# Attention with pooled queries: another spread of the value products over the steps, and two turning steps moved

## The chip, the core and the metric

The kernel runs on one core of a Trainium2 chip. The metric is the device time of one execution in microseconds (us), as the median of several runs. TensorE (PE) multiplies matrices into PSUM, VectorE (DVE), ScalarE (ACT) and GpSimd (POOL) work element by element, and SyncE (SP) issues the DMAs. Each engine takes its own instructions in the order of the program and waits on semaphores for what it needs from the others.

## The reference

Attention is followed by a dense layer and a layer of eight experts; the change touches the attention alone.

```
q_pool = q.reshape(B, H, S // 2, 2, D).mean(axis=3)       # B 2, H 8, S 1152, D 64
scores = (1 / sqrt(D)) * q_pool @ k.T                     # 576 x 1152 for each head
attn   = softmax(scores)                                  # row maximum taken off, divided by row sums
x      = (attn @ v), heads side by side                   # 1152 x 512
x      = mish(x @ w_in) @ w_out                           # hidden size 2048
P      = exp(x @ w_gate), then 8 rounds of rows and columns divided by their sums
out    = sum over e of P[:, e] * (relu(x @ w1[e]) @ w2[e])
```

All is float32. The kernel splits operands into a high and a low part and adds two or three products of the parts.

## The kernel before

**Pairs and steps.** The 16 heads are worked in 8 pairs (`p` from 0 to 7). A pair has 2 x 576 = 1152 pooled query rows, that is nine tiles of 128 (`t` from 0 to 8); the middle tile, t = 4, holds rows of both heads. One pass of the loop `for g in range(...)` (L686) is one step, g = 9 p + t; below, "step t" is the step of that number in any pair. A step works on three query tiles at once:

- `scores(g)` (L443): TensorE multiplies the tile's queries with the keys, six matmuls of 384 columns (twelve in step 4) into the one buffer `psS` (three PSUM banks). VectorE then negates, moves the result to a tile `e` and takes the row minimum in the same instruction (L458). So the next step's scores wait until that instruction has ended. `e` has three buffers.
- `exps(g)` (L472) on ScalarE, at the end of the step. One step later `hand_over` (L478) has SP copy `e` to a tile `er` of another format by DMA; the buffer of `e` is free again only when that DMA has landed.
- `transposes(g - 3)` (L535): nine transposes of the tile `er` of three steps before, three to a PSUM buffer `psT` (there are four); ScalarE copies each as the high part `eth` (L538), VectorE writes the low part `etl` (L541).

**Products with the values.** The turned tiles are gathered in four groups of a pair, 256, 320, 320 and 256 queries. A group is full after the transposes of step 4, of step 7, of step 0 of the next pair and of step 2 of the next pair. A full group puts 18 matmuls into the list `av_todo` (L556); `run_av(n)` issues up to n of them. All groups use the one buffer `psA`. With the last of the 18 comes the emptying: a copy on ScalarE (`avt`, L565) and a sum on VectorE (`xs`, L570); until the sum has ended, the next group's first product waits. In pairs 1 to 7 the table `AV` (L612) says how many products a step issues ahead of its transposes and how many behind them (only those that were listed before the step's own transposes); in pair 0 each step issues up to nine, behind the transposes.

**Turning keys and queries.** The table `TURN` (L613) says in which steps TensorE turns keys and queries to the layout that scores need. `trans_k` (L386) turns a third of one head's keys: three transposes to a `psT` buffer, and a copy on ScalarE (L392). Step numbers under `k0` are for the next pair's first head, under `k1` for the pair's own second head, which scores need from step 4 on (in pair 0 `k10` holds instead of `k1`). `trans_q` (L428) turns up to four query tiles: the transposes, a copy on ScalarE (`qT`, L435), and then, listed in `loads` and so issued by SP at the beginning of the next step, the two DMAs of `swap` (L426), which put the halves of the 128 partitions the other way round into a second slot. Under `q` stand the steps of its three parts: the first, of tiles 0 to 3, is done for the next pair, whose step 0 reads it, the other two for the pair's own. Every query tile is used in both slots: the first matmul of a tile's scores reads the first slot, the second one the swapped slot.

**Order within a step** (L692 to L726): listed loads; `scores`; GpSimd's splitting of the next heads (`prep`); the first turning item, if there is one; the first part of the products; the transposes; the hand-over of the step before; the second part of the products; the other turning items; `exps`. ScalarE and VectorE get their copies and sums in the same order.

**Beside it**, DMAs load the next heads' q, k and v (`qraw`, `kraw`, `vraw`) and the weights of the dense layer, whose splitting on VectorE, ScalarE and GpSimd is planned by step number. After 72 steps the dense layer and the experts follow, in which TensorE has work nearly all the time.

Of the kernel before, what the change touches and what calls it, by code (L numbers as in the profile page):

```python
# [23 lines left out]
def pool_attention_mish_sinkhorn_kernel(  # L24
# [22 lines left out]
    NPAIR = B * H // 2  # L47
# [57 lines left out]
    def run(t, eng, most=99):  # L105

        q = queue[eng]
        while q and q[0][0] <= t and most > 0:
            q.pop(0)[1]()
            most -= 1  # L110
# [180 lines left out]
    with ExitStack() as actx:  # L291
        def pool(name, bufs, **kw):
            return actx.enter_context(tc.tile_pool(name=name, bufs=bufs, **kw))
# [27 lines left out]
        for i in range(2):  # L321
            t = z_p.tile([P, 2, 2, P], F32R, name=f"qz{i}")
# [25 lines left out]
        def split_kv(p, j, which, eng, part, more=True):  # L348
            if p == NPAIR:
                return  # L350
            raw = raws[which, p, j]
            pl, dst = (kst_p, kst) if which == "k" else (vst_p, vst)
            if part == 0:
                t = dst[p, j] = pl.tile([P, NK, 2, D], F32R, tag=which + "st", name=f"{which}st{p}_{j}")
                split_hi(eng, t[:, :, 0, :], raw)
            else:
                t = dst[p, j]
                split_lo(eng, t[:, :, 1, :], raw, t[:, :, 0, :])
                p, j = (p, 1) if j == 0 else (p + 1, 0)
                if more and p < NPAIR:  # L360
                    loads.append(lambda: load_kv(p, j, which))
# [24 lines left out]
        def trans_k(p, j, c3):  # L386
            if c3 == 0:
                kT[p, j] = kt_p.tile([P, S], F32R, tag="kT", name=f"kT{p}_{j}")
            ps = ps_t.tile([P, 4, P], F32R, tag="t", name=f"psk{p}_{j}_{c3}")
            for i in range(3):  # L390
                nc.tensor.transpose(ps[:, i, :], kst[p, j][:, 3 * c3 + i].rearrange("p a d -> p (a d)"), identr)  # L391
            nc.scalar.activation(  # L392
                kT[p, j][:, c3 * TH:(c3 + 1) * TH],
                ps[:, 0:3, :].bitcast(F32).rearrange("p a d -> p (a d)"), AF.Copy)
# [15 lines left out]
        def trans_q0(u):  # L410

            n = min(2, QTL - 2 * u)
            ps = ps_t.tile([P, 2, 2, P], F32R, tag="t", name=f"psq0_{u}")
            for i in range(n):
                for s in range(2):
                    nc.tensor.transpose(
                        ps[:, i, s, :], qst[0][:, 2 * u + i, s:s + 2, :].rearrange("p a d -> p (a d)"), identr)
            t, i = q_tile(0, 2 * u)
            nc.scalar.activation(t[:, i:i + n], ps[:, 0:n].bitcast(F32), AF.Copy)
            if 2 * u <= MID < 2 * u + n:  # L420
                middle(0, ps[:, MID - 2 * u], 2)
# [6 lines left out]
        def trans_q(p, u):  # L428
            ps = ps_t.tile([P, 4, P], F32R, tag="t", name=f"psq{p}_{u}")
            t, _ = q_tile(p, 4 * u)  # L430
            n = min(4, QTL - 4 * u)
            for i in range(n):
                nc.tensor.transpose(
                    ps[:, i, :], qst[p][:, 4 * u + i, 0:2, :].rearrange("p a d -> p (a d)"), identr)
            nc.scalar.activation(t[:, :, 0, :], ps[:, 0:n].bitcast(F32), AF.Copy)  # L435
            loads.append(lambda: swap(t))
            if 4 * u == MID:
                middle(p, ps, 1)
                loads.append(lambda: swap(qz[p % 2]))
# [22 lines left out]
        def exps(g):  # L462
            p, t = divmod(g, QTL)
            sc, nm = scS.pop(g)
            sc = sc.rearrange("p a b -> p (a b)")
            if g < 2:
                e = erS[g] = er_p.tile([P, S], F32, tag="er", name=f"er{g}")
            else:
                e = eS[g] = sc
            if t == 0:  # L470
                rsS[p] = tiny.tile([P, QTL], F32, tag="rs", name=f"rs{p}", bufs=2)
            nc.scalar.activation(e, sc, AF.Exp, bias=nm, scale=-1.0, accum_out=rsS[p][:, t:t + 1])  # L472
# [115 lines left out]
        def run_av(n):  # L588
            for _ in range(n):
                if av_todo:  # L590
                    av_todo.pop(0)()

        NQ = NPAIR * QTL
# [15 lines left out]
            "k00": 3, "k01": 4, "k10": 7, "k11": 8,  # L609
        }  # L610
        PREP0 = {"k00": 3, "k01": 3, "q0": 4, "q1": 4, "q2": 5, "q3": 5, "v10": 5, "v11": 7, "k10": 7, "k11": 8}
        AV = [(0, 9), (0, 8), (0, 8), (2, 7), (0, 4), (7, 4), (0, 6), (8, 0), (0, 9)]  # L612
        TURN = {"k0": (5, 6, 7), "k1": (2, 3, 3), "k10": (0, 0, 2), "q0": (2, 2, 3), "q": (6, 1, 2)}  # L613

# [8 lines left out]
        q0, q1, q2 = slice(0, 2), slice(2, 4), slice(4, QTL)  # L625
# [36 lines left out]
        def prep(p, t):  # L662
            for x, at_ in (PREP if p else PREP0).items():
                if at_ == t:
                    if x[0] == "q":
                        split_q(p + 1, nc.gpsimd, int(x[1]))
                    else:
                        split_kv(p + (x[0] == "k"), int(x[1]), x[0], nc.gpsimd, int(x[2]))

        def turn(p, t):  # L670
            fs = []
            for j in range(2):
                pp = p + (j == 0)
                if pp < NPAIR:
                    fs += [
                        lambda pp=pp, j=j, c=c: trans_k(pp, j, c)
                        for c in range(3) if TURN["k10" if p == 0 and j == 1 else f"k{j}"][c] == t]
            for u in range(3):
                pp = p + (u == 0)
                if p == 0 and TURN["q0"][u] == t:  # L680
                    fs.append(lambda u=u: trans_q0(u + 2))
                if 0 < pp < NPAIR and TURN["q"][u] == t:
                    fs.append(lambda pp=pp, u=u: trans_q(pp, u))
            return fs

        for g in range(T0 + EARLY):  # L686
            p, t = divmod(g, QTL)
            if g == 1:
                bctx.close()
                ps_t = pool("ps_t", 4, space=PSUM)  # L690
                ps_a = pool("ps_a", 1, space=PSUM)
            pre = turn(p, t) if g < NQ else []  # L692
            waiting, loads[:] = loads[:], []
            for f in waiting:
                f()
            if g < LAG:
                exps(g)
                for f in pre:
                    f()
                if g + 1 < LAG:  # L700
                    split_kv(0, 0, "v", nc.gpsimd, g)
                    scores(g + 2, ps_s)
            else:
                if LAG < g < NQ:
                    scores(g)
                if p and g < NQ:
                    prep(p, t)
                if g < T0:
                    run(g, "dve")
                if pre:  # L710
                    pre.pop(0)()
                spread = 0 < p < NPAIR
                if spread:
                    run_av(AV[t][0])
                ready = len(av_todo)
                if g < NQ + LAG:
                    transposes(g - LAG)
                if g <= NQ:
                    hand_over(g - 1)
                if not p:  # L720
                    prep(p, t)
                run_av(min(ready, AV[t][1] if spread else 9 if g < NQ else 18))
                for f in pre:
                    f()
                if g < NQ:
                    exps(g)  # L726
            if p and t == 0:
                row_sums(p - 1)
            if p and t == 1:
                turn_sums(p - 1)  # L730
            if late:
                late.pop(0)()
            if g < T0:
                run_all(g)
            if g == QTL:
                load_gate()
            if g == NQ - 1:
                sctx.close()
                ps_o = ctx.enter_context(tc.tile_pool(name="ps_o", bufs=3, space=PSUM, side="right"))
                wpools["d0"] = ctx.enter_context(tc.tile_pool(name="wd0", bufs=1, side="right"))  # L740
                mctx = ExitStack()
                wpools["d1"] = mctx.enter_context(tc.tile_pool(name="wd1", bufs=1, side="right"))
                wpools["t"] = mctx.enter_context(tc.tile_pool(name="wt2", bufs=3, side="right"))
            if g >= T0:
                mish_step(g - T0)
# [50 lines left out]
    for s in range(NS):  # L796
        for th in range(NTH):
            last = max(k for k, b in enumerate(BANKS) if b[:2] == (s, th))
            ready = max(last + 2, NB - 1 if s == NS - 1 else 9 if s == 1 else 0)
# [492 lines left out]
```

## Time and profile before

| | |
|---|---|
| median of 3 runs | 1235.37 us (1233.79 to 1235.45) |
| the profiled execution | 1235.16 us, of which its span 1233.3 us |
| TensorE, busy share of the span | 98% |
| VectorE, ScalarE, GpSimd | 69%, 48%, 51% |
| attention, first to last scores | 6.65 to 263.7 us |
| one pair of heads, steps 0 to 8 (pairs 1 to 6) | 32.1 to 35.0 us |

The span runs from the first to the last instruction; the run's time has 1.9 us more. Over the whole span TensorE is the engine with the least room, but in the attention, the first fifth, three engines are near 85 to 92% busy (TensorE, VectorE, ScalarE), and the DMA engines near 78%. There the chain of waits goes from one engine to another within each step, so the place to look at is the step and not the share.

### The profile page before, as it was taken

The page shows a single profiled execution, that of the slowest core. Times are in us where ns is not written, and L with a number is a line of the kernel's source. Part 1 is how long each engine was busy: PE and PEld are TensorE (multiplying, and loading weights), DVE is VectorE, ACT ScalarE, POOL GpSimd, SP SyncE. Part 2 cuts the span into 40 slices and gives each one's busy share as a digit, 9 for nine tenths or more (in the row PEclk, how much of TensorE's full clock was granted, in tenths as well). Part 3 has the DMA queues.
Part 4 walks back from the last instruction along what each step waited for, and adds up shares of the span by engine and source line. Part 5 has one row for each costly group of instructions (what it writes and reads, how often), then busy time and mean ns, then how long its engine had stood idle before and what let it go on. Part 6 is the DMA issues. An engine that isn't in the chain of part 4 may idle for free.

```text
span 1233.3 us, 19334 instructions
## 1 busy us (share of the span) xinstructions
PE 1209.1 (98%) x6840; PEld 1114.4 (90%) x6840; DVE 854.4 (69%) x1588; ACT 596.9 (48%) x1364; POOL 623.7 (51%) x704
## 2 busy tenths in 40 slices
PE   8999999999999999999999999999999999999998
PEld 8988888989999999898888899998888899998887
DVE  7888889876534433777866767866866767866865
ACT  7888888878454443452322333333322333333331
POOL 5545565415444422374755665555455565555452
PEclk9999999999999999999999999999999999999999
DMA  6877777654222311011111111111111111111112
GB/s 203 278 255 259 254 263 258 221 188 130 86 86 72 97 34 30 1 52 25 39 49 53 46 49 52 52 52 31 37 45 52 51 45 52 53 52 34 39 39 77
DMA packets 67551, 116.84 MB, mean 95 GB/s; under 512 B 7224, under 2 KB 39808, under 8 KB 67456
## 3 DMA queue, kind: packets, MB, share of 16 engines
q1 hardware_dynamic: 67456, 115.62, 29.6%
q8 instruction: 54, 0.88, 0.3%
q14 instruction: 41, 0.34, 0.1%
HBM read 66.86 MB, written 2.40 MB: 56 GB/s over the span
## 4 chain that ended last, share of the span: by engine, by line
PE 89%; DVE 7%; ACT 2%; issue 1%; DMA 0%; SPq 0%; POOL 0%; ACTq 0%; DVEq 0%
PE po L1196 30%; PE c L1038 26%; PE ph L224 10%; PE po L777 8%; PE psS L453 5%; PE psA L556 5%; DVE e L458 3%; PE psT L535 2%; DVE etl L541 2%; DVE xs L570 1%; ACT e L472 1%; ACT eth L538 1%; PE psk L391 1%; PE pg L832 0%; ACT kT L392 0%
## 5 line engine op out<-in xcount | busy, mean ns | idle before, releaser
L81 POOL TENSOR_TENSOR wslotsl<-s,wslotsh 128x256 fp32r<-128x256 f32 x180 | 132.3, 743 | 238.5 <-ACT wslotsh L74 238.5
L1204 DVE SCALAR_TENSOR_TENSOR oacc<-po,Pm,oacc 128x512 f32<-128x512 f32 (+1 forms) x217 | 161.2, 747 | 103.5 <-PE po L1196 96.9
L1196 PE MATMUL po<-wdbl,hhall 128*128 128x512 f32 (+1 forms) x543 | 214.4, 395 | 0.0
L1196 PE MATMUL po<-wdbh,hlall 128*128 128x512 f32 (+1 forms) x543 | 214.1, 394 | 0.0
L1196 PE MATMUL po<-wdbh,hhall 128*128 128x512 f32 (+1 forms) x543 | 214.0, 394 | 0.0
L1055 ACT ACTIVATE t<-c 128x384 f32<-128x384 f32 x80 | 39.1, 489 | 247.3 <-PE c L1038 247.3
L1075 ACT ACTIVATE hhall<-c 128x384 fp32r<-128x384 f32 x180 | 88.5, 492 | 129.1 <-DVE c L1071 126.4
L1196 PEld LDWEIGHTS po<-wdbh,hhall 128*128 128x128 f32 x543 | 102.0, 188 | 24.4
L1196 PEld LDWEIGHTS po<-wdbh,hlall 128*128 128x128 f32 x543 | 102.0, 188 | 23.3
L1196 PEld LDWEIGHTS po<-wdbl,hhall 128*128 128x128 f32 x543 | 102.0, 188 | 23.3
L458 DVE TENSOR_SCALAR_CACHE_REDUCE e<-psS 128x1152 f32<-128x1152 f32 x72 | 97.2, 1351 | 30.2 <-PE psS L453 24.3
L81 POOL TENSOR_TENSOR wslotsl<-rawu,wslotsh 128x256 fp32r<-128x256 f32 x120 | 90.6, 769 | 51.2 <-ACT wslotsh L74 51.2
L541 DVE TENSOR_TENSOR etl<-psT,eth 128x384 fp32r<-128x384 f32 (+1 forms) x240 | 108.1, 507 | 5.5 <-ACT eth L538 4.2
L1076 DVE SCALAR_TENSOR_TENSOR hlall<-c,hhall 128x384 fp32r<-128x384 f32 x180 | 98.7, 548 | 2.1
L538 ACT ACTIVATE eth<-psT 128x384 fp32r<-128x384 f32 (+1 forms) x240 | 93.3, 478 | 8.1 <-PE psT L535 7.5
L1038 PE MATMUL c<-x2h,wslotsl 128*128 128x384 f32 x280 | 94.8, 338 | 0.0
L1038 PE MATMUL c<-x2h,wslotsh 128*128 128x384 f32 x280 | 94.5, 337 | 0.0
L1038 PE MATMUL c<-x2l,wslotsh 128*128 128x384 f32 x280 | 94.1, 336 | 0.0
L556 PE MATMUL psA<-etl,vst 128*128 128x256 f32 (+1 forms) x288 | 83.4, 311 | 10.5 <-DVE xs L570 10.0
L472 ACT ACTIVATE e<-e,nm 128x1152 f32<-128x1152 f32 x70 | 89.1, 1273 | 1.3 <-ACT eth L538 1.2
L453 PE MATMUL psS<-kT,qT 128*128 128x384 f32 x384 | 82.1, 348 | 4.9 <-DVE e L458 4.7
L74 ACT ACTIVATE wslotsh<-s 128x256 fp32r<-128x256 f32 x180 | 72.0, 411 | 24.3 <-DVE s L1004 24.3
(358 smaller groups left out, 3048.1 us busy)
## 6 DMA issues: line engine op xcount, KB each, us to landing
er<-e SPq DMA_DIRECT2D x70, 576.0 KB, 3.6
rawd<-in_moe_w_dram SPq DMA_DIRECT2D x60, 256.0 KB, 2.8
rawu<-in_moe_w_dram SPq DMA_DIRECT2D x30, 384.0 KB, 3.3
raw<-in_moe_w_in_dram SPq DMA_DIRECT2D x16, 512.0 KB, 4.2
raw<-in_moe_w_out_dram SPq DMA_DIRECT2D x16, 512.0 KB, 3.7
vraw<-in_v_dram SPq DMA_DIRECT2D x16, 288.0 KB, 3.5
kraw<-in_k_dram SPq DMA_DIRECT2D x15, 288.0 KB, 4.4
qraw<-in_q_dram SPq DMA_DIRECT2D x7, 576.0 KB, 6.9
```

What stands on the lines that cost most here:

```text
L81: eng.tensor_tensor(out=lo, in0=src, in1=hi.bitcast(F32), op=ALU.subtract)
L224: nc.tensor.matmul(ps[:, 0:TH], lhsT=a, rhs=b, start=(n == 0), stop=(n == len(ops) - 1))
L453: nc.tensor.matmul(ps[:, kb, 0:TH], lhsT=a, rhs=kt[:, kb * TH:(kb + 1) * TH], start=(n == 0), stop=(n == len(ops) - 1))
L458: nc.vector.tensor_scalar(sc, ps[:, :, 0:TH], -1.0, None, op0=ALU.mult, op1=ALU.min, accum_out=nm)
L472: nc.scalar.activation(e, sc, AF.Exp, bias=nm, scale=-1.0, accum_out=rsS[p][:, t:t + 1])
L538: nc.scalar.activation(eh[:, cs, o:o + b - a], ps[:, 0:3, a:b], AF.Copy)
L541: nc.vector.tensor_tensor(out=el[:, cs, o:o + b - a], in0=ps[:, 0:3, a:b], in1=eh[:, cs, o:o + b - a].bitcast(F32), op=ALU.subtract)
L556: nc.tensor.matmul(box["ps"][:, 0:n], lhsT=vst[p, j][:, c].rearrange("p a d -> p (a d)"), rhs=(el, eh)[which][:, c, 0:n], start=(c == 0 an ...
L1038: nc.tensor.matmul(cb[c], lhsT=a_, rhs=b_, start=FIRST[n] and m == 0, stop=LAST[n] and m == len(ops) - 1, skip_group_check=True)
L1076: los.append(lambda: nc.vector.scalar_tensor_tensor(out=lo, in0=b, scalar=0.0, in1=hi.bitcast(F32), op0=ALU.max, op1=ALU.subtract))
L1196: nc.tensor.matmul(ps[:, 0:w], lhsT=a, rhs=b[:, cs], start=(n == 0), stop=(n == len(ops) - 1))
L1204: nc.vector.scalar_tensor_tensor(out=oa, in0=ps[:, 0:w], scalar=gate, in1=oa, op0=ALU.mult, op1=ALU.add)
```

## The change

The table `AV` goes. In every step of every pair `run_av` issues up to nine products, all behind the transposes, and only those listed before the step's own transposes. So a group's 18 products fall on the two steps after the one that fills it: step 5 and 6, 8 and 0, 1 and 2, 3 and 4, and step 7 issues none. Before, the counts of steps 0 to 8 were 9, 8, 8, 9, 4, 11, 6, 8, 9; a group's last product fell in steps 0, 3, 5 and 7, and in steps 3, 5 and 7 it stood ahead of the transposes.

One third of the second head's keys is turned in step 0 instead of step 2, and one in step 2 instead of the second of step 3. The first part of the next pair's queries is turned in step 7 instead of step 6; there it is the second item, behind the transposes.

```diff
-        AV = [(0, 9), (0, 8), (0, 8), (2, 7), (0, 4), (7, 4), (0, 6), (8, 0), (0, 9)]
-        TURN = {"k0": (5, 6, 7), "k1": (2, 3, 3), "k10": (0, 0, 2), "q0": (2, 2, 3), "q": (6, 1, 2)}
+        TURN = {"k0": (5, 6, 7), "k1": (0, 2, 3), "k10": (0, 0, 2), "q0": (2, 2, 3), "q": (7, 1, 2)}
...
-                spread = 0 < p < NPAIR
-                if spread:
-                    run_av(AV[t][0])
                 ready = len(av_todo)
                 if g < NQ + LAG:
                     transposes(g - LAG)
...
-                run_av(min(ready, AV[t][1] if spread else 9 if g < NQ else 18))
+                run_av(min(ready, 9 if g < NQ else 18))
```

## Rows read from the trace of the kernel before

**Rows 1.** The page, part 1: busy time, share, instructions of TensorE.

```profile
PE 1209.1 (98%) x6840; PEld 1114.4 (90%) x6840; DVE 854.4 (69%) x1588; ACT 596.9 (48%) x1364; POOL 623.7 (51%) x704
```

**Rows 2.** Windows of one pair each (two of eight): length, then busy us by engine.

```profile
core 0: us, PE busy (x) PEld busy (x) DVE busy (x) ACT busy (x) POOL busy (x), PEclk, DMA share, GB/s
...
132.18:165.79 33.61, 31.02 (x242) 29.84 (x242) 28.62 (x60) 29.04 (x66) 20.10 (x20) 1.00 0.78 261
165.79:199.05 33.26, 31.03 (x243) 29.66 (x242) 28.71 (x59) 28.64 (x64) 19.47 (x19) 1.00 0.78 257
```

**Rows 3.** Waits of TensorE, 33 to 270 us: sum, times, longest.

```profile
PE psA L556 <- DVE xs L570: 10.0, 14, 1.3
PE psS L453 <- DVE e L458: 2.3, 10, 0.4
PE psT L535 <- ACT kT L392: 1.9, 5, 0.5
```

**Rows 4.** Chain in order of time, 120 to 170 us: start, us, what.

```profile
133.52 0.73 PE psT L535 x9
134.25 1.39 PE psA L556 x9
...
144.23 1.37 DVE e L458 x2
145.59 0.64 DVE wt L162
...
146.26 0.49 DVE xs L570
```

**Rows 5.** Timeline, steps 2 and 3 of pair 4: start, us, engine line, [idle before].

```profile
141.06 0.71 PE L535 MATMUL psT<-identr,er 128*128 128x128 f32 x6 [0.44 <-ACT kT L392]
...
146.80 0.39 PE L556 MATMUL psA<-etl,vst 128*128 128x256 f32 x1 [1.32 <-DVE xs L570]
```

**Rows 6.** Timeline of SP, 150 to 161 us.

```profile
151.40 0.49 SPq L478 DMA_DIRECT2D er<-e  x1
152.00 0.54 SPq L345 DMA_DIRECT2D qraw<-in_q_dram  x1
...
154.99 3.54 SPq L478 DMA_DIRECT2D er<-e  x2
```

**Rows 7.** Timeline, steps 7 and 8 of pair 4.

```profile
159.11 0.60 ACT L435 ACTIVATE qT<-psq 128x512 fp32r<-128x512 f32 x1 [0.26 <-PE psq L433]
159.73 1.32 SPq L426 DMA_DIRECT2D qT<-qT  x2
...
161.09 1.36 DVE L458 TENSOR_SCALAR_CACHE_REDUCE e<-psS 128x1152 f32<-128x1152 f32 x1 [1.25 <-DMA er<-e]
161.26 0.88 PE L535 MATMUL psT<-identr,er 128*128 128x128 f32 x9
161.93 1.45 ACT L538 ACTIVATE eth<-psT 128x192 fp32r<-128x192 f32 x6
162.22 0.50 SPq L478 DMA_DIRECT2D er<-e  x1
162.51 1.32 PE L453 MATMUL psS<-kT,qT 128*128 128x384 f32 x6 [0.36 <-DVE e L458]
162.78 0.58 SPq L337 DMA_DIRECT2D vraw<-in_v_dram  x1
164.78 1.43 POOL L81 TENSOR_TENSOR kst<-kraw,kst 128x576 fp32r<-128x576 f32 x1
```

**Rows 8.** Timeline of TensorE: first scores of step 8 in pairs 3 and 5.

```profile
128.64 0.42 PE L453 MATMUL psS<-kT,qT 128*128 128x384 f32 x1
...
195.78 0.44 PE L453 MATMUL psS<-kT,qT 128*128 128x384 f32 x1
```

**Rows 9.** Line L426 in steps 6 to 8 of pairs 3 and 5.

```profile
L426 SPq DMA_DIRECT2D qT<-qT x2: 633/634/635, 126.4 to 127.1; - x2
...
DMA to landing us min/median/max: 2.5/2.5/2.5
...
L426 SPq DMA_DIRECT2D qT<-qT x2: 633/634/635, 193.2 to 193.9; - x2
...
DMA to landing us min/median/max: 3.4/3.4/3.4
```

## The prediction, made before the changed kernel ran

> **What bounds the kernel now.** I read the page's busy shares first: over the whole span TensorE is at 98% [rows 1], so what shortens or lengthens its road through the attention moves the end by the same amount; behind the attention nothing changes. Then the windows by pair: a pair takes 33.6 and 33.3 us in the two shown, with TensorE busy 31.0, ScalarE 29.0 and 28.6, VectorE 28.6 and 28.7 [rows 2]. No engine is full; some 2.5 us in each pair are waits that go round between the engines, and the reader is to look for who makes TensorE wait. Three waits hold nearly all of it: the first product of a group waits for the sum that empties `psA` (10.0 us in 14 waits, two in each of pairs 1 to 7), scores wait for the row minimum of the step before (2.3 us), and a transpose waits for the copy of a turned third of keys (1.9 us) [rows 3].
>
> The chain in order of time shows how the largest comes about. In step 3 the last two products of a group stand ahead of the transposes, and the sum `xs` that empties `psA` stands on VectorE behind the row minimum (1.37 us) and a weight instruction (0.64 us) [rows 4]; TensorE idles 1.32 us before the next group [rows 5]. The timeline shows such a wait in step 3 seven times, 0.68, 1.30, 1.30, 1.32, 1.30, 1.32 and 0.77 us, together 8.0. The other 2.0 of the 10.0 us are the waits of step 5.
>
> Step 7 has another limit. Its row minimum starts 1.25 us late, since it needs the buffer of `e` that a hand-over frees on landing, and the scores of step 8 wait for its end at 162.51 [rows 7]. That hand-over was issued at 154.99, behind the one of 151.40 and the 576 KB of q from 152.00 [rows 6]. Pairs 1 to 5, which all load q at this place, show such a late start, by 0.35 to 1.25 us.
>
> **Part by part.** The sum is made against the profiled execution, 1235.16 us (span 1233.3 and 1.9 around it); the median of the runs is 0.2 us above it.
>
> *Step 3.* Each group now ends with the last products of step 2, 4, 6 or 0, and the next begins behind the following transposes (two steps on, for the group that begins in step 8). Between the two lie scores, a turning item and the transposes, 2.0 us and more (transposes alone take 0.73 [rows 4]), while the copy and the sum take 0.9, and the sum is on VectorE ahead of the next row minimum. So the wait of step 3 goes: −8.0 us. What is late next there is the row minimum of step 3, which ends some 0.6 us before the scores of step 4 want it. Bounds: −8.0, and −6.0 if ScalarE, which now does the group's copy in step 2 too, eats 0.3 us of each.
>
> *Step 5.* Its wait for `psA` goes too (2.0 us), and so do most waits for the row minimum there (about 0.2 in each of seven pairs, 1.4 in all), since step 4 now has nine products instead of four. But in pairs 1 to 5 the stretch from step 4's transposes to step 8's scores ends with the landing of that hand-over. The three large transfers ahead of it are issued at the same places as before, so I take the landing, and with it step 8, as unmoved, and count only pairs 6 and 7: −0.9. Bounds: 0 and −3.4.
>
> *Counts.* Nine products of 320 columns take 1.39 us [rows 4], 0.15 each. Steps 0 to 3 now issue 36 instead of 34 of a pair's 72, and a wide product in place of a narrow one: +0.27 us in each of seven pairs, +1.9. Steps 4 to 7 issue two fewer, hidden by the landing in five pairs, −0.5 in the other two. Together +1.4; bounds 0 and +1.9.
>
> *Keys turned earlier.* The three transposes and the copy go from step 3 to step 0, another three from step 3 to step 2 in place of those: the same work for TensorE (0.2 us) and ScalarE (0.5 us), no DMA, no other queue. New is that step 0 needs the second head's split keys; GpSimd ends them at 166.21 [rows 7], and the transposes would come 1.1 us behind the scores' start at 165.79 [rows 2], at 166.9. The cover is 0.7 us, and it grows, because GpSimd's work on `xs` now begins a step earlier. I take 0; if the cover were gone, the whole splitting of 1.43 us [rows 7] in each pair, 10 us. Whether a transpose of step 2 still waits for the keys' copy (0.44 us in one, 1.9 us in five [rows 3, 5]) depends on ScalarE's lead, which loses nothing there between step 1 and the copy: 0, bounds −1.9 and +1.9.
>
> *Queries turned later.* Here is the new wait. In step 6 the copy `qT` ended at 159.71 and SP issued the first of the two swaps at 159.73, 2.8 us ahead of step 8's scores [rows 7]; in pairs 3 and 5 it was 2.2 us (126.4 against 128.64) and 2.6 us (193.2 against 195.78) [rows 8, 9]. In step 7 the four transposes come behind those of the step. These start when the hand-over has landed, together with the row minimum, which holds step 8's scores for 1.42 us. The copy is queued on ScalarE behind the six `eth` of that step (1.45 us, the first some 0.35 us behind the transposes' start), then takes 0.60 [rows 7], and SP can issue the first swap 2.4 us after the landing, 1.0 us behind step 8's scores. So it comes 3.2 us later in pair 3, 3.6 in pair 5.
>
> On SP it is now queued behind a hand-over and a load of v (162.22 and 162.78 [rows 7]), and so are its bytes. What waits is the second matmul of step 0's scores, and behind it on TensorE everything. Room before: in pair 3 the second swap lands at 127.1 + 2.5 = 129.6 [rows 9] and the second matmul is due at 132.35 (scores 132.18 [rows 2]): 2.7 us. In pair 5 it lands at about 197.0, and is due at 199.2: 2.2 us. Lateness: pair 3, 3.2 − 2.7 = 0.5 with its own 2.5 us to landing, 1.4 with the 3.4 us that swaps took in pair 5; pair 5, 3.6 − 2.2 = 1.4. A step-7 swap has more bytes ahead of it than either, so I take 1.4, at seven pair boundaries (step 0 of pairs 1 to 7): +9.8. Bounds: 0.5 each, 3.5, and 2.2 each, 15.4, if ScalarE's `exps` of step 6 delays the copy by another 0.8 us.
>
> The Trainium skill, "DMA: Bandwidth & Descriptors", section "Anatomy of one DMA", gives a transfer about 2.0 us plus its bytes at 436 GB/s; for the 128 KB of a swap that is an estimate of 2.3 us, below the 2.5 and 3.4 of this trace. By the page the lateness would be 0.3 us, the term +2.1 and the sum −5.4. The rows decide, since 3.4 was measured with other transfers ahead.
>
> **Sum.** −8.0 − 0.9 + 1.4 + 0 + 9.8 = +2.3 us: 1237.5 in a profiled execution, 1237.7 as a median.
>
> **Rivals.**
>
> *A, faster: the swap is hardly late.* If it lands 2.5 us after issue, as in pair 3, the seven waits cost 3.5: −8.0 − 0.9 + 1.4 + 3.5 = −4.0, 1231.4. For it: in pairs 3 and 5 the wait would come only to 0.5 with that landing. Against it: one hand-over and one load stand ahead of it in the queue. It decides below 1.07 us per boundary, where the gains (8.0 + 0.9 − 1.4 = 7.5 over seven) are used up. This is also where the skill's formula leads.
>
> *B, clearly slower: ScalarE delays the copy.* Step 6 now ends with a group's copy `avt` before its `exps`, and step 7 has the keys' copy, six `eth`, `qT` and `exps`, 4 us on ScalarE. If the `eth` of step 7 start 0.8 us after the landing, the lateness is 2.2: −8.0 − 0.9 + 1.4 + 15.4 = +7.9, 1243.3. Against it: the landing itself leaves ScalarE time to catch up.
>
> *C, no change: what TensorE loses at step 0 comes back.* While it waits, ScalarE and VectorE catch up, the waits of step 2 go (−1.9), and the sum is +0.4: 1235.8. For it: ScalarE works without a gap from step 1 to the copy in step 2 in the timeline. Against it: the same chain runs on from step 0 however late that starts.
>
> **How the numbers follow.** About 0.2%, 2.5 us, is what a measurement of this kernel can tell from no change. Chances: forecast 0.42, A 0.24, B 0.14, C 0.20. The forecast's own range is 1235.5 to 1241. The range reaches to A's 1231 and past B's 1243, to 1245 for the upper bounds of the counts and of step 2. Faster (below 1232.9): nearly all of A, 0.23. Slower (above 1237.9): B, and somewhat less than two thirds of the forecast and a little of C, 0.42. Between them: 0.35.
>
> **What would show it.** The wait of `psA` on `xs` in steps 3 and 5 gone; a new wait of TensorE at `psS`, released by the DMA `qT<-qT`, of 1 to 2 us at the second matmul of step 0 in pairs 1 to 7; step 8's scores still released by the row minimum, at an unmoved distance from step 4's transposes in pairs 1 to 5; the transposes in step 0 not waiting for `kst`. The prediction is wrong if that swap lands in time, if step 8's scores come earlier by 0.5 us or more in pairs 1 to 5, or if another wait takes the place in step 3.

## The result, and the profile after

The changed kernel takes 1246.59 us (median of four runs, 1243.91 to 1249.62), the kernel before 1235.35 beside it: a ratio of 1.0095, interval 1.0069 to 1.0120. It is 11.2 us slower; 1237.7 was forecast, with a range from 1231 to 1245. The profiled execution took 1245.79 us, its span 1244.0.

All of it lies in the attention. From the start of the last scores to the end both executions take the same, 970.9 us before and 970.6 after. So the waits of TensorE in the attention come first, as sum, times and longest; the window is longer, since the attention is.

```profile
PE psS L453 <- DMA qT<-qT: 17.1, 7, 3.5
PE psT L535 <- DMA er<-e: 6.4, 6, 1.7
PE psq L433 <- ACT kT L392: 0.8, 1, 0.8
PE psS L453 <- DVE e L458: 0.8, 1, 0.8
PE psA L556 <- DVE rs L482: 0.5, 1, 0.5
```

Against [rows 3] the 10.0 us of `psA` on `xs` are gone, and so is the wait for the keys' copy in step 2. In their place stand 17.1 us on the swap, once in each of seven pairs, and 6.4 us, nearly all in step 7, where the transposes now stand idle before a hand-over's landing.

The lengths of the steps, from the start of one step's scores to the next's, tell what each wait was worth. The table is worked out from the timelines: means over pairs 2 to 6, in us. The rows below the second are experiments, told further down.

| kernel | 0 | 1 | 2 | 3 | 4 | 5 | 6 | 7 | 8 | pair |
|---|---|---|---|---|---|---|---|---|---|---|
| before | 3.24 | 3.83 | 4.01 | 5.02 | 3.80 | 4.01 | 3.12 | 3.26 | 3.50 | 33.78 |
| after | 7.37 | 3.57 | 3.57 | 3.23 | 3.95 | 3.17 | 3.17 | 4.06 | 3.30 | 35.39 |
| queries in step 6 again | 3.41 | 3.67 | 3.61 | 3.23 | 3.95 | 3.17 | 3.75 | 3.34 | 3.39 | 31.53 |
| nine alone | 3.16 | 4.01 | 3.84 | 3.44 | 4.03 | 3.17 | 3.65 | 3.14 | 3.40 | 31.83 |
| swap first | 4.37 | 3.52 | 3.57 | 3.23 | 3.95 | 3.17 | 3.17 | 4.02 | 3.30 | 32.30 |

Step 0 has grown by 4.1 us, step 3 has shrunk by 1.8. The cores' view and the windows of pairs 3, 4 and 5 (columns as in [rows 2], the granted clock third from the end) show a second thing, which the waits do not tell:

```profile
core: us from the first to the last instruction, mean granted TensorE clock
core 0: 1244.0 us, clock 0.993
```

```profile
105.95:141.26 35.31, 31.51 (x244) 30.53 (x242) 28.52 (x61) 28.28 (x66) 18.45 (x19) 0.95 0.75 247
141.26:175.29 34.03, 30.24 (x244) 29.33 (x242) 28.43 (x60) 28.25 (x66) 20.48 (x21) 1.00 0.77 253
175.29:212.27 36.98, 31.62 (x243) 30.73 (x242) 28.14 (x60) 28.37 (x65) 20.05 (x20) 0.95 0.72 235
```

Pairs 3 and 5 have a mean granted clock of 0.95, where [rows 2] have 1.00. Inside a pair it falls at the wait for the swap. Here is step 0 of pair 5, where that wait ended at 179.14; the last window is at 0.50, that is at 1.2 instead of 2.4 GHz:

```profile
175.00:179.20 4.20, 0.68 (x6) 0.42 (x4) 1.23 (x3) 2.17 (x5) 4.20 (x5) 1.00 0.95 276
179.20:180.30 1.10, 1.10 (x8) 1.06 (x9) 0.01 (x1) 0.00 (x0) 0.10 (x1) 1.00 0.37 147
180.30:183.70 3.40, 3.40 (x21) 3.40 (x19) 2.96 (x6) 1.66 (x4) 0.00 (x0) 0.50 0.29 112
```

In pairs 2 and 3 it had fallen before the wait ended, at 71.74 and 108.94:

```profile
71.10:77.90 6.80, 6.16 (x28) 6.10 (x29) 2.96 (x6) 1.75 (x5) 1.35 (x1) 0.50 0.44 168
108.64:112.05 3.41, 3.12 (x17) 3.05 (x17) 1.14 (x1) 0.80 (x3) 1.22 (x1) 0.50 0.41 153
```

The chain in order of time through that place (start, us, what) is the one the prediction drew, link by link, with one link of another size:

```profile
163.81 6.68 DMA er<-e
170.49 0.14 issue
170.62 0.44 PE psT L535 x3
...
171.09 0.56 ACT eth L538 x3
...
171.73 0.80 ACT eth L538 x3
172.53 0.50 ACT qT L435
...
173.04 0.64 SPq L426
...
173.74 5.27 DMA qT<-qT
179.01 0.14 issue
179.14 1.11 PE psS L453 x5
180.26 0.22 PE psk L391 x3
180.48 1.17 PE psT L535 x9
181.64 2.39 PE psA L556 x9
```

The hand-over lands, the transposes and the six `eth` follow, then the copy, then the swap. The second swap takes 5.27 us to land. The last line shows the half clock: nine products take 2.39 us, against 1.39 in [rows 4].

What stood ahead of that swap is in SP's timeline (start, us), here at the ends of pair 4 and of pair 6:

```profile
171.63 0.46 SPq L478 DMA_DIRECT2D er<-e  x1
172.19 0.54 SPq L337 DMA_DIRECT2D vraw<-in_v_dram  x1
173.04 1.33 SPq L426 DMA_DIRECT2D qT<-qT  x2
...
241.73 0.58 SPq L337 DMA_DIRECT2D vraw<-in_v_dram  x1
243.76 1.31 SPq L426 DMA_DIRECT2D qT<-qT  x2
```

At the end of pair 4 the load of v was issued 0.8 us ahead of the swap. At the end of pair 6 it was issued 2.0 us ahead; there the swap landed in 2.5 us, and the wait was the shortest of the seven, 0.9 us.

### The profile page after: what moved, and what is told of

The parts are those of the page before. It is cut to its first block, busy times and chain, and to the rows that moved or that the text cites. A ratio compares the mean times of both kernels' runs of the same rounds, so it can differ in the third digit from the quotient of the medians.

```text
span 1244.0 us, 19311 instructions
## 1 busy us (share of the span) xinstructions
PE 1209.3 (97%) x6840; PEld 1118.8 (90%) x6840; DVE 852.2 (69%) x1588; ACT 593.6 (48%) x1364; POOL 624.2 (50%) x704
## 4 chain that ended last, share of the span: by engine, by line
PE 90%; DMA 5%; ACT 2%; DVE 1%; issue 1%; SPq 0%; POOL 0%; ACTq 0%; POOLq 0%; DVEq 0%
PE po L1192 30%; PE c L1034 25%; PE ph L224 10%; PE po L773 8%; PE psA L556 5%; PE psS L453 5%; PE psT L535 3%; DMA er<-e 3%; DMA qT<-qT 2%; ACT e L472 1%; ACT eth L538 1%; PE psk L391 1%; SPq L426 0%; PE psw L618 0%; PE pg L828 0%
## 5 line engine op out<-in xcount | busy, mean ns | idle before, releaser
L453 PE MATMUL psS<-kT,qT 128*128 128x384 f32 x384 | 84.1, 352 | 20.5 <-DMA qT<-qT 17.1
L453 PEld LDWEIGHTS psS<-kT,qT 128*128 128x128 f32 x384 | 66.2, 193 | 24.5 <-issue 12.2
```

The lines of the kernel that those rows point to most:

```text
L453: nc.tensor.matmul(ps[:, kb, 0:TH], lhsT=a, rhs=kt[:, kb * TH:(kb + 1) * TH], start=(n == 0), stop=(n == len(ops) - 1))
```

## The experiments

The theory, W: the loss is the wait of step 0 on the swap, and behind it the half clock; nine products per step save time by themselves. Rivals: nine per step costs by itself (S), the keys' move costs (K). All times stand beside 1235.0 to 1235.2 us of the kernel before.

**Queries back in step 6.**

```diff
-        TURN = {..., "q": (7, 1, 2)}
+        TURN = {..., "q": (6, 1, 2)}
```

> The changed kernel with one part undone: the first part of the next pair's queries is turned in step 6 again; nine products per step and the keys stay as changed. Theory W (the whole loss is the wait of step 0 on the swap and the half clock that follows it; nine products per step save about the 7.5 us that the prediction counted): no wait of psS on the DMA qT<-qT, granted clock 1.00 through the attention, 1227 to 1231 us. Rival S (nine products per step cost time by themselves, because step 7 has nothing left to fill the landing of the hand-over, 6.4 us of waits in the changed kernel's trace): 1235 us or more, with those 6.4 us unchanged.

1223.97 us, ratio 0.9908 (0.9893 to 0.9923). No wait on the swap; the waits for a hand-over were 5.3 us. One stretch of 3.4 us was still at half clock, in pair 1, behind waits of 1.3 us (a hand-over) and 0.5 us (a row minimum); the other three executions have mean clocks of 0.997 to 0.999. S has fallen: with nine per step the kernel beats the one before by 11 us, more than I expected. The queries' move alone costs 1246.59 − 1223.97 = 22.6 us.

**Only the queries moved**, in the kernel before.

```diff
-        TURN = {..., "q": (6, 1, 2)}
+        TURN = {..., "q": (7, 1, 2)}
```

> The kernel before with one part of the change alone: the first part of the next pair's queries turned in step 7; spread of the products and the keys as before. Theory W: seven waits of psS on qT<-qT, 14 to 19 us together, some followed by a stretch at half clock, 1250 to 1258 us. Rival S (the wait is mostly slack that the kernel before spends elsewhere, in steps 2, 3 and 5): the waits of step 3 and 5 shrink by what step 0 gives ScalarE and VectorE to catch up, 1238 to 1245 us.

1258.60 us, 1.0185 (1.0168 to 1.0202). Its waits of TensorE:

```profile
PE psS L453 <- DMA qT<-qT: 19.5, 7, 3.5
PE psA L556 <- DVE xs L570: 10.0, 14, 1.3
PE psS L453 <- DVE e L458: 1.5, 8, 0.2
PE psT L535 <- ACT kT L392: 0.8, 4, 0.2
```

The same wait with the old spread, 19.5 us, and six stretches at half clock. The 10.0 us of `psA` have not shrunk at all: what TensorE loses in step 0 is not given back in steps 3 and 5. The waits for the row minimum (2.3 to 1.5 us) and for the keys' copy (1.9 to 0.8) did become shorter, by 1.9 us together. The two ways round agree: 22.6 us with the new spread, 1258.6 − 1235.2 = 23.4 with the old one.

**Only the keys moved**, in the kernel before.

```diff
-        TURN = {"k0": (5, 6, 7), "k1": (2, 3, 3), ...}
+        TURN = {"k0": (5, 6, 7), "k1": (0, 2, 3), ...}
```

> The kernel before with one part of the change alone: thirds of the second head's keys turned in steps 0, 2, 3 instead of 2, 3, 3. Theory W and the prediction: no difference, 1234 to 1237 us; no wait of psk for kst in step 0. Rival K (the copy of 0.5 us in step 0 lengthens ScalarE's chain through steps 0 to 2): 1238 to 1240 us, with the wait of psT on the keys' copy above the 1.9 us of before.

1233.51 us, 0.9991 (0.9982 to 1.0000): a little faster or the same. The wait for the keys' copy went from 1.9 us to 0.6. K has fallen.

**Useless products in the wait.**

```diff
+            if p and t == 0:
+                for n in range(4 if p == NPAIR - 1 else 12):
+                    nc.tensor.matmul(ps[:, 0, 0:TH], lhsT=identr, rhs=kT[p, 0][:, 0:TH], start=True, stop=True)
             for kb in range(3):
```

> The changed kernel with useless work in the wait: ahead of step 0's scores TensorE does twelve products of 384 columns (some 2.0 us; four in pair 7) into the buffer that the scores then overwrite. The wait on the swap stays where it ends, but TensorE is busy for most of it. Theory C (the half clock behind the wait costs 5 to 8 us of the 11): granted clock 1.00 through the attention, waits of psS on qT<-qT 3 to 6 us instead of 17.1, 1237 to 1241 us. Rival N (steps behind the wait are held by other engines, so the half clock costs little): 1244 to 1248 us.

1245.60 us, 1.0085 (1.0056 to 1.0113), and inconclusive as a test of the clock: 9.7 us of waits were left behind the twelve products, and the clock still fell in two of the seven step 0s, and once more behind a wait of 1.9 us for a hand-over at the end of the attention. The profiled execution is the slowest of the four: 1250.24 us at a mean clock of 0.996, beside 1247.31 at 0.997 and 1243.89 and 1242.39 at 1.000. And the same step stands at both clocks in one execution. Step 0 of pairs 3, 6, 4 and 5:

```profile
106.10:112.93 6.83, 5.02 (x28) 4.64 (x28) 2.97 (x6) 1.64 (x4) 3.71 (x4) 0.75 0.58 199
211.41:218.27 6.86, 5.07 (x29) 4.75 (x28) 2.97 (x6) 2.23 (x6) 3.24 (x4) 0.75 0.42 156
143.33:147.61 4.28, 3.67 (x28) 3.34 (x28) 2.17 (x4) 1.64 (x4) 3.77 (x4) 1.00 0.52 185
177.45:182.33 4.88, 3.65 (x29) 3.33 (x28) 2.17 (x5) 1.64 (x4) 3.73 (x4) 1.00 0.62 199
```

In windows as in [rows 2], TensorE is busy 5.02 and 5.07 us at a mean clock of 0.75, and 3.67 and 3.65 at 1.00: one stretch at half clock costs 1.4 us. In the changed kernel's trace the same difference, step 0 less its wait against the 3.65 of pairs 4 and 6, is 1.4 + 2.4 + 1.3 + 1.4 = 6.5 us for four stretches (that of pair 2 is twice as long, 6.8 us). The 17.1 us of waits leave 5.5 of the 22.6 open, which agrees with it within the scatter of the runs.

**The swap issued ahead of the load of v.**

```diff
-            loads.append(lambda: swap(t))
+            if u == 0:
+                loads.insert(0, lambda: swap(t))
+            else:
+                loads.append(lambda: swap(t))
```

> The changed kernel, with the swap of the first query part listed ahead of step 8's other loads, so that SP issues it ahead of the load of v instead of behind it. ScalarE's copy still holds its issue at 1.0 us behind step 8's scores. Theory B (the swap lands 4.1 to 5.3 us after issue, instead of the 3.4 of the prediction, because the bytes of a hand-over and of a load of v are ahead of it): it lands about 1 us earlier, seven waits of 8 to 12 us together instead of 17.1, fewer stretches at half clock, 1234 to 1240 us. Rival L (what delays it is older: the backlog of the hand-overs, or one late DMA engine): waits of 15 us or more, 1243 us or more.

1228.39 us, 0.9950 (0.9934 to 0.9965), better than expected. SP's timeline (L481 is the hand-over here) and line L426 at pair 4's end, two views:

```profile
159.44 0.46 SPq L481 DMA_DIRECT2D er<-e  x1
160.85 1.32 SPq L426 DMA_DIRECT2D qT<-qT  x2
162.22 0.60 SPq L337 DMA_DIRECT2D vraw<-in_v_dram  x1
```

```profile
DMA to landing us min/median/max: 2.5/2.5/2.5
```

The swap is issued as late as before, 1.0 us behind step 8's scores (159.83), but lands in 2.5 us instead of 4.1 to 5.3: the 288 KB of v in front of it cost 1.6 us or more. The waits are 0.6 to 1.0 us each, 5.5 in all, and in the profiled execution the clock stays at 1.00. It is 18.2 us less, for 11.6 us less waiting; the other 6.6 are near the 6.5 worked out for the half clock. (Of the other three executions the two with a mean clock of 0.998 took as long as this one, and that with 0.997 took 2.2 us more, so some time at half clock can cost next to nothing.) Rival L has fallen.

**Both turning items ahead of step 7's transposes.**

```diff
-                if pre:
-                    pre.pop(0)()
+                for f in pre[:2 if t == 7 else 1]:
+                    f()
+                del pre[:2 if t == 7 else 1]
```

> The changed kernel, with step 7 unchanged in its content but both turning items ahead of the transposes: the queries' transposes and their copy then do not stand behind the landing of the hand-over and the six eth. Theory P (the place behind the transposes makes the swap late, not the step): the swap is issued some 1 to 2 us ahead of step 8's scores, no wait or under 0.5 us at each step 0, granted clock 1.00, 1223 to 1228 us. Rival T (step 7 is too late anywhere): waits of 1 us or more each, 1232 us or more.

1245.47 us, 1.0087 (1.0069 to 1.0106): a miss. ScalarE's copy now ends at 170.8, ahead of the `eth`, but SP shows:

```profile
171.10 0.47 SPq L478 DMA_DIRECT2D er<-e  x1
171.66 0.54 SPq L337 DMA_DIRECT2D vraw<-in_v_dram  x1
172.30 1.53 SPq L426 DMA_DIRECT2D qT<-qT  x2
```

The swap is listed for step 8, and SP gets to it only behind step 7's hand-over, which waits for the transposes, and behind the load of v. So it came 0.8 us behind step 8's scores all the same. Its place was held twice, by ScalarE's order and by SP's, and I had seen only the first as decisive.

**The same, with the swap issued at once**, in step 7, ahead of the hand-over.

```diff
-            loads.append(lambda: swap(t))
+            if u == 0:
+                swap(t)
+            else:
+                loads.append(lambda: swap(t))
```

> The run with both turning items of step 7 ahead of the transposes, and the swap of the first query part now issued by SP in step 7 itself, ahead of the hand-over, instead of at the beginning of step 8 behind a hand-over and a load of v. Theory Q (after that run's swaps came 0.8 us behind step 8's scores all the same, what held them was SP's order): the swap is issued 1 us or more ahead of step 8's scores and lands in under 3 us, no wait of psS on qT<-qT, granted clock 1.00, 1222 to 1226 us. Rival T (step 7 is too late anywhere, since ScalarE's copy or the load of q's bytes hold it): waits of 1 us or more at most boundaries, 1230 us or more.

1225.06 us, 0.9916 (0.9900 to 0.9933), no wait on the swap. It was issued between 2.1 us ahead of step 8's scores and 0.2 behind them, less early than expected in four of seven cases, and landed in under 3 us. Step 7 is not too late as such. The swap now goes ahead of the load of v too, so this run does not part the earlier issue from the shorter queue. (One stretch of 6.8 us was at half clock in the trace, at the end of pair 5, behind a wait of 1.9 us for a hand-over.)

**Nine products per step alone.**

```diff
-        TURN = {..., "k1": (0, 2, 3), ..., "q": (7, 1, 2)}
+        TURN = {..., "k1": (2, 3, 3), ..., "q": (6, 1, 2)}
```

> Nine products per step alone: keys and queries turned in the steps of before. With the run where only the queries are undone (1223.97 us) it gives what the keys' move is worth. Theory W: the keys are worth little, 1223.5 to 1226 us, the wait of psT on the keys' copy in step 2 at 0 to 2 us. Rival K (the gain of 11 us needs the keys in step 0): 1229 us or more.

1222.79 us, 0.9901 (0.9885 to 0.9916): 12.4 us faster than before, without the keys' move, so K has fallen here too. Its waits:

```profile
PE psS L453 <- DVE e L458: 4.3, 9, 0.8
PE psT L535 <- DMA er<-e: 2.4, 5, 0.8
PE psA L556 <- DVE rs L482: 0.5, 1, 0.5
```

**Another spread**, with queries in step 6 and the keys as changed.

```diff
-        AV = [(0, 9), (0, 8), (0, 8), (2, 7), (0, 4), (7, 4), (0, 6), (8, 0), (0, 9)]
-        TURN = {"k0": (5, 6, 7), "k1": (2, 3, 3), ...}
+        AV = [(0, 9), (0, 9), (0, 9), (0, 5), (0, 13), (0, 9), (0, 5), (4, 0), (0, 9)]
+        TURN = {"k0": (5, 6, 7), "k1": (0, 2, 3), ...}
```

> A version that may beat both: queries in step 6, keys as changed, and the products spread 9, 9, 9, 5, 13, 9, 5, 4 (ahead of the transposes), 9 over steps 0 to 8, so that each group still ends a step before the next begins, and four products go from step 3 to the stretch from step 4's transposes to step 8's scores. Theory D (that stretch ends with a landing, so what is added to it is hidden): 0.5 us less in each of seven pairs than the run with queries undone, 1220 to 1222 us, waits of psT on er<-e below 3 us. Rival F (those four products delay step 4 or step 7 as much as they relieve step 3): 1223.5 us or more.

1222.03 us, 0.9894 (0.9878 to 0.9909), 13.2 us faster than the kernel before and the lowest of the series, though its interval overlaps that of nine alone. Against the run with queries in step 6, step 3 became 0.38 us shorter in the mean of pairs 2 to 6, and steps 4 to 7 together only 0.09 longer, so the four products are hidden there, and the waits for a hand-over fell to 1.6 us, both as expected; but steps 0 and 8 became 0.3 us longer, and a pair takes 31.49 us against 31.53. The 1.9 us by which its median is lower are not settled as a gain of the spread, since the other run had a stretch at half clock in its trace and this one none.

The same spread with the keys of before:

> The spread 9, 9, 9, 5, 13, 9, 5, 4, 9 with keys and queries both turned in the steps of before. If the keys' move costs the 1.2 us by which the two runs with nine products per step differ (1223.97 with it, 1222.79 without), 1220.5 to 1221.5 us; if that difference is the scatter between runs, 1221.5 to 1223 us, as with the keys moved (1222.03).

1222.87 us, 0.9899 (0.9884 to 0.9914): the keys' move is lost in the scatter. Against nine alone, 1222.79 with keys and queries in the same steps and a mean clock of 1.000 in all executions of both, the other spread is worth nothing that these runs can tell.

## Why the prediction was wrong, point by point

**Queries turned later: the step that failed.** The prediction took "1.4, at seven pair boundaries", +9.8 us. The sign, the place and the chain were right, and the swap was issued 1.0 us behind step 8's scores in five of seven cases, as worked out (1.4 in the other two). Two sizes were wrong. The landing was put at 3.4 us; that of the second swap was 4.1 to 5.3 in six cases, in which the load of v was issued 0.8 us ahead of the swap (1.4 in one of the six). In the seventh, where it was issued 2.0 us ahead, it was 2.5, and with the swap first it was 2.5 everywhere. The text had named those bytes and then added nothing for them to the longer of two landings at the old place. That made 17.1 us of 9.8. And at four of the seven waits the clock fell: the prediction had no term for it, and the workings above give 5.5 to 6.6 us. The move measured 22.6 in all. The waits of 1.3 us that the kernel before shows had left the clock at 1.00 [rows 2, 5], and that was taken, without a word, to hold for any wait. One reading in the term was off as well: by [rows 9] the second swap of pair 5 lands at 193.9 + 3.4 = 197.3, not at 197.0, which would have made the term 1.7 us at each boundary, +11.9.

The formula of the Trainium skill ("DMA: Bandwidth & Descriptors", "Anatomy of one DMA") gave an estimate of 2.3 us; the section states it for transfers that GpSimd issues, and this one is issued by SP. With only a hand-over ahead the trace has 2.5, so it is close there; it has no term for what is queued ahead, and that decided.

**Step 3, step 5, counts: −7.5 forecast, −12.4 measured** (nine alone). Over pairs 1 to 7 of the two traces step 3 gave −9.9 us (−8.0 forecast), steps 4 to 7 −1.8 (−1.4), steps 0 to 2 +0.1 (+1.9). Step 3 lost 1.58 us per pair where 1.3 of idle time were seen. The timelines of pair 4 put the rest on TensorE's own work: the transposes and nine products of step 3 take 2.18 us before, idle time taken off, and 1.91 with nine alone, where all nine have 256 columns and stand together. The +1.9 was over-counted by little (the two products more in steps 0 to 3 both have 256 columns, 0.12 us each, so 1.7), and it did not come, since the wait for the keys' copy in step 2 (1.9 us [rows 3]) went at the same time; steps 0 to 2 together are 0.07 us shorter in the mean of pairs 2 to 6. Why that wait went is not shown.

**Step 8 unmoved: right.** Steps 4 to 7 last 14.19 us before, 14.35 after and 13.99 with nine alone, in the mean. In the changed kernel step 8's scores came between 0.3 us earlier and 0.6 later in pairs 1 to 5, counted from step 4's scores. The landing in step 7 holds that stretch, as said: with 6.4 us of new waits there it is only 0.16 us per pair longer.

**Keys turned earlier: right**, 0 forecast, −1.7 measured alone, +1.2 and −0.8 in the other two comparisons, all within the scatter. The +1.2 need not be the keys' at all: the run with the keys moved has a mean clock of 0.997 to 0.999 in its four executions, nine alone 1.000. No wait for `kst` appeared in the changed kernel; in the other spread with the keys moved there was one, of 0.6 us.

**The rivals.** A (the swap hardly late) is what the run with the swap first came near to, with its 5.5 us of waits. B had the right outcome by the wrong cause: the DMA queue made the swap late, not ScalarE, and the clock added the rest. C (what is lost at step 0 comes back) is refuted as an outcome by the kernel with only the queries moved: some 1.9 us of waits went there, as C had it, beside 19.5 us of new ones.

The three parts, each measured alone in the kernel before, add up to −12.4 − 1.7 + 23.4 = +9.3, against the +11.2 that the change did; the 1.9 us between them are not explained. The loss is one moved step, and it hid a gain that was larger than forecast.

## What to carry to other kernels

A transfer's landing is priced by what its issuing queue and the DMA queue have ahead of it at its new place, in order and in bytes, not by what it took at its old one. A copy that must be issued by another engine has two orders that can hold it, and moving it in one of them alone may change nothing. Where TensorE gets new waits, the clock around them is a term of the sum, above all where they are longer than any that the trace shows: ask it of a row, or carry it as an unknown with a bound.

## What the runs showed of the hardware that I had not expected

TensorE's granted clock fell to 0.50 (1.2 GHz) at waits of 2.61 to 3.52 us in four of seven cases of the changed kernel, and stayed at 1.00 behind waits of 2.35 and 2.39 us. The length of one wait does not settle it. With queries back in step 6 it fell behind waits of 1.29 and 0.47 us; with useless products it fell behind waits of 1.81 and 1.79 us and not behind one of 2.23; with both turning items ahead of the transposes it stayed at 1.00 behind a wait of 3.25. What does settle it was not tested. A stretch at 0.50 lasted 3.4 us, or 6.8. In the changed kernel it began between 0.6 us before the wait's end (pair 2) and 1.2 us after it (pair 5).

Executions differ in how much of it they have. The changed kernel's times spread over 5.7 us at mean clocks of 0.990 to 0.993; those of nine alone, at 1.000 in all four, over 1.2.
